# Moving one matrix-product piece, one weight unit and a few additions in a fused top-k attention and MLP kernel

## The chip, the core and the metric

The kernel runs on one core of a Trainium2 chip. The metric is the device time of one execution in microseconds (us). Beside the time of each execution there is a profile of one of them, taken by the hardware profiler; its span runs from the first to the last instruction.

The engines are called as in the profile: PE is the matrix engine (PEld its weight loads), DVE the vector engine, ACT the scalar engine, POOL the GpSimd engine, SP the engine that issues most DMAs.

## The reference: what is computed

For 8 batches and 8 heads, with 576 rows and a head dimension of 64, all in float32:

```
scores = q @ k.T / 8                       # 576 x 576 for each head
kth    = 32nd largest of each row
attn   = softmax(where(scores >= kth, scores, -1e9))
x      = (attn @ v), heads side by side    # 4608 x 512
out    = gelu(x @ w_in) @ w_out            # w_in 512 x 2048, w_out 2048 x 512, exact gelu
```

## The kernel before: how the work is tiled and ordered

**Items and slots.** The attention is cut into items. An item is one tile of 128 query rows for a pair of heads (both heads side by side, 2 x 576 scores per row). A batch has four head pairs and four full row tiles, which makes 16 full items, and two items that hold the leftover 64 rows of two pairs each. So there are N = 144 items. They are ordered so that two row tiles of a pair follow each other, then the next pair: after eight full items, 256 rows of x are complete over all heads. Even batches put their two leftover items behind the full ones, odd batches ahead of them.

The program is one loop over slots n (from line 1034). In slot n each engine gets, in this order of the program: the addition that completes a unit of weights (POOL), scores of item n+2 (in late slots of two items, n+2 and n+3, in every second slot), `attend(n-3)`, which is the product with v of two row tiles at once and so exists in every second slot, `copy_x`, which copies that product to `xT` on ACT, the softmax of item n-1 on ACT, the transposes of item n-2 on PE with the copies to `pt` on ACT, and the top-k of item n on DVE. At the end POOL computes the thresholds and normalises item n-1 (line 507); the transposes of the next slot need that. Every engine works through its own instructions in program order, so this order is the schedule. Every engine pair is tied only by data.

**The MLP in between.** The MLP runs in pieces that are strewn into the slots by `mlp(count)`. A piece is two matmuls 128x256 of a first layer block (`l1_piece`, line 673, tile `h_ps`), or one matmul 128x512 or two matmuls 128x256 of a second layer block (lines 755, 773/776, 809/811, tiles `y_ps` and `seven`). A first layer block has eight pieces, a second layer block seven or eight. `room_in(n)` says how many pieces slot n may take: 4 in all slots up to 11 (START is 10), later a block's size plus or minus one. A piece of the first layer has a `need`: the tokens of x that must be complete. `mlp` stops where `need` is above `ready[0]`, and `ready[0]` is raised to the finished tokens at fixed places of the slot. In a slot with a product that completes 256 tokens, the next first layer block is still blocked directly after the product. There the loop does something else: with `few[0]` (slots from 13) it issues the eight main transposes of item n-2 at once (`turned`, made by `turn_both`, line 553) and the small transposes of the leftover keys (`tails`, line 527), and only then raises `ready[0]`.

**The second layer** saves products by sums of quarters (one multiplication in eight is saved). `sums` (lines 699 to 708) makes three sums of the gelu result `g` and changes one quarter of `g` in place, in four POOL additions into one buffer `sum`; `trio_piece` and `seven_piece` use them. `last_parts` (line 881) adds up the last 256 rows of the output on DVE and stores them.

**The weights** come as 16 units. A unit is loaded by SP, taken apart on ACT (lines 205 and 206, and a multiplication by a constant, on ACT at line 212 or, for slots 11 to 18, on DVE at line 208) and added up on POOL (line 227) at the beginning of its slot. `SLOT_OF` gives the units, in the order `ORDER`, the slots 1 to 10 and 13 to 18. The size steps of a slot's unit are issued at the end of the slot before.

**At the beginning** the PE has little to do; `keep_busy` fills slots below 10 with matmuls on constants (line 995), whose results nobody reads. From slot 10 the MLP starts.

Of the kernel before, what the change touches and what calls it, by code (L numbers as in the profile page):

```python
# [14 lines left out]
def kernel(  # L15
# [19 lines left out]
    nc = tc.nc  # L35
    f32, i32, u32 = mybir.dt.float32, mybir.dt.int32, mybir.dt.uint32
# [5 lines left out]
    P = 128  # L42
# [115 lines left out]

    SLOT_OF = dict(zip(ORDER, [*range(1, START + 1), *range(START + 3, START + 9)]))
    UNIT_IN = {n: u for u, n in SLOT_OF.items()}
    unit_in = UNIT_IN.get

# [53 lines left out]
    def waits(u):  # L218

        return u == ORDER[-1]  # L220
# [104 lines left out]
    def pair_tile(name, tag="pr"):  # L325
        return ps.tile([P, 2, 512], f32, tag=tag, bufs=1, name=name)
# [31 lines left out]
    def scores(i, second=False):  # L358
        if i >= N or i in S_of:
            return  # L360
        pair, t = items[i]
        S_of[i] = s = work.tile([P, 2 * S], f32, tag="s", bufs=6, name="s")
        s_ps = pair_tile("s_ps", "l1" if second else "pr")
        if not few[0]:
            last_keys(i, bank("t_ps"))()
        if t < NM:
            q_t, kt = q_of[pair][:, t * P : (t + 1) * P], kt_of[pair]
            for e in range(2):
                rows = slice(e * D, (e + 1) * D)
                nc.tensor.matmul(  # L370
                    s_ps[:, e], lhsT=q_t[rows, :], rhs=kt[rows, 0:SM], start=True, stop=True
                )
            if i == 0:

                nc.scalar.activation(s[:, 0:SM], s_ps[:, 0], func=AF.Copy, scale=scale)
                nc.scalar.activation(s[:, S + TL :], s_ps[:, 1], func=AF.Copy, scale=scale)  # L376
                return
            nc.scalar.activation(spread(s, S + TL, SM), s_ps, func=AF.Copy, scale=scale)  # L378
        else:

            for r in range(2):
                kt = kt_of[pair + r]
                for e in range(2):
                    rows = slice(e * D, (e + 1) * D)
                    nc.tensor.matmul(
                        s_ps[half(r, e), r, :], lhsT=kt[rows, SM + P + e * TL : SM + P + (e + 1) * TL],
                        rhs=kt[rows, 0:SM], start=True, stop=True,
                    )
            s2 = s.rearrange("p (r n) -> p r n", r=2)
            nc.scalar.activation(s2[:, :, 0:SM], s_ps, func=AF.Copy, scale=scale)  # L390
# [122 lines left out]
    def transposes(i):  # L513

        if i < 0 or i >= N:
            return []
        t, s = items[i][1], S_of.pop(i)
        pr = [None]

        def tails(ahead):  # L520
            tp = bank("tp_t")
            keys = last_keys(ahead, tp) if ahead is not None and ahead < N else None
            at = P
            if t % 2 == 0:
                pt_now[0] = work.tile([P, 2 * NM + 1, 2 * P], f32, tag="pt", bufs=1, name="pt")
            if t < NM:
                nc.tensor.transpose(tp[:, at : at + P], s[:, SM : S + TL], ident)  # L527
            else:
                for r in range(2):
                    nc.tensor.transpose(  # L530
                        tp[0:TL, at + r * P : at + (r + 1) * P],
                        s[:, r * S + SM : (r + 1) * S], ident,
                    )
            if keys:
                keys()
            if t < NM:
                nc.scalar.copy(
                    out=pt_now[0][:, 2 * NM, t % 2 * P : (t % 2 + 1) * P], in_=tp[:, at : at + P]
                )
                return  # L540
            for e in range(2):
                c = slice(e * TL, (e + 1) * TL)
                nc.scalar.copy(
                    out=halves(pt_end[c, 0, :], e, P),
                    in_=halves(tp[0:TL, at : at + 2 * P], e, P),
                )

        x = t % 2 * P if t < NM else 0

        def turn_over(tp, e):  # L550
            first = e * (S + TL if t < NM else S)
            for j in range(NM):
                nc.tensor.transpose(  # L553
                    tp[:, j * P : (j + 1) * P], s[:, first + j * P : first + (j + 1) * P], ident
                )

        def main(e):
            tp = bank("tp")
            turn_over(tp, e)
            nc.scalar.copy(  # L560
                out=pt_now[0][:, e * NM : (e + 1) * NM, x : x + P],
                in_=tp.rearrange("p (j n) -> p j n", j=NM),
            )

        def turn_both():
            pr[0] = tp = pair_tile("tp")
            for e in range(2):
                turn_over(tp[:, e], e)

        def both():  # L570
            if pr[0] is None:
                turn_both()
            tp = pr[0]
            nc.scalar.copy(  # L574
                out=pt_now[0][:, 0 : 2 * NM, x : x + P],
                in_=tp.rearrange("p e (j n) -> p (e j) n", j=NM),
            )

        if few[0]:
            return [tails, lambda _: both(), turn_both]  # L580
        return [tails] + [lambda _, e=e: main(e) for e in range(2)]

    def copy_x():
        while copies:
            copies.pop()()
# [112 lines left out]
    def sums(u):  # L698

        g = g_of[u].rearrange("p x (f n) -> p x f n", f=2)  # L700
        a11, a21, a12, a22 = (g[:, :, f, h * P : (h + 1) * P] for f in range(2) for h in range(2))
        t = work.tile([P, 2, 3, P], f32, tag="sum", bufs=1, name="sum")
        s1, s2, s4 = (t[:, :, x] for x in range(3))
        nc.gpsimd.tensor_tensor(s1, a21, a22, op=ALU.add)
        nc.gpsimd.tensor_tensor(s2, s1, a11, op=ALU.subtract)
        nc.gpsimd.tensor_tensor(a21, a11, a21, op=ALU.subtract)
        nc.gpsimd.tensor_tensor(s4, a12, s2, op=ALU.subtract)
        sums_of[u] = t

    def weight_sums(j):  # L710
# [32 lines left out]
    def part_tile():  # L743
        return work.tile([P, HALF], f32, tag="part", bufs=3, name="part")
# [137 lines left out]
    def last_parts(tok, k, a):  # L882

        dve, add = nc.vector.tensor_tensor, ALU.add
        if k == 0:
            end_of["y"] = y0, y1 = y_tile(), y_tile()
            nc.scalar.copy(out=y0[:, B1], in_=a[:, 0])
            end_of["a"] = a
            return
        y0, y1 = end_of["y"]  # L890
        s7 = y7[0]
        if k == 1:
            dve(y0[:, B2], a[:, 0], y0[:, B1], op=add)
            dve(y0[:, B1], end_of["a"][:, 1], y0[:, B1], op=add)
            nc.sync.dma_start(out=out[last_row : last_row + P, B1], in_=y0[:, B1])
            dve(s7, s7, y0[:, B2], op=add)
            dve(y1[:, B2], a[:, 1], s7, op=add)
            nc.sync.dma_start(out=out[last_row + P : last_row + 2 * P, B2], in_=y1[:, B2])
            dve(y0[:, B2], a[:, 1], y0[:, B2], op=add)
            return  # L900
        dve(y0[:, B2], a[:, 1], y0[:, B2], op=add)
        nc.sync.dma_start(out=out[last_row : last_row + P, B2], in_=y0[:, B2])
        dve(y1[:, B1], s7, a[:, 0], op=ALU.subtract)
        nc.scalar.dma_start(out=out[last_row + P : last_row + 2 * P, B1], in_=y1[:, B1])
# [68 lines left out]
    def room_in(n):  # L973

        x = n - START - 1
        if x < 1:
            return 4
        if x >= len(sizes):
            return 0
        return sizes[x] + (1 if x % 2 == 0 else -1)  # L980
# [53 lines left out]
    for n in range(ahead):  # L1034

        left[0] = room_in(n)
        few[0] = n > START + 2
        eager[0] = n > N
        if not waits(unit_in(n)):
            weights_add(unit_in(n))  # L1040
        larger(n + 1)
        for piece in squares_in.pop(n, []):
            piece()
        two = few[0] and n % 2 == 0 and n + 3 < N and items[n + 3][1] < NM
        scores(n + 2, two)
        if two:
            scores(n + 3)
        product = attend(n - 3)
        late = n > START
        if n <= START:  # L1050

# [2 lines left out]
        if waits(unit_in(n)):  # L1054
            weights_size(unit_in(n))
            weights_add(unit_in(n))
        mlp(1)
        if few[0] and n % 2:
            run_gelus()
        tr = transposes(n - 2)  # L1060
        turned = tr.pop() if few[0] and tr else None
        if product and n > START and done[0] < len(pieces) and pieces[done[0]][0] > ready[0]:

            if turned:
                turned()
            for piece in tr[:1]:
                piece(n + 2 if few[0] else None)
            tr, ready[0] = tr[1:], n_tok[0]
# [103 lines left out]
```

## Time and profile before

| what | us |
|---|---|
| median of 3 runs (1547.71 to 1549.83) | 1548.0 |
| profiled execution, its own time | 1547.88 |
| its span, first to last instruction | 1546.1 |
| PE busy in the span | 1513.3 |
| DVE busy | 1336.4 |
| ACT busy | 1160.4 |
| POOL busy | 1142.8 |

A row of the timeline gives the start, the length, the engine, the line, the operation with the tiles that it writes and reads, its shape and a count, and in brackets how long the engine had been idle before and what released it. Consecutive equal instructions are merged into one row. A float32 matmul is recorded as two instructions, so a first layer piece of two matmuls shows as x4 in the trace. The time between two matmul rows is read from start to start, because the ends are modelled and overlap the next start.

### The profile page before, as it was taken

Reading aid. Unit: us, or ns where it says so; the run is one execution under the profiler, and the core shown is the slowest. Engines: PE = TensorE matmul, PEld = TensorE weight load, DVE = VectorE, ACT = ScalarE, POOL = GpSimd, SP = SyncE. Lnnn points to the kernel's source line nnn. Section 1 sums busy time; section 2 is a strip of 40 time slices with the busy share of each in tenths; the row PEclk is TensorE's granted clock in tenths of the full one; section 3 lists DMA queues with packets and bytes.
Section 4 is the critical chain, followed back from the end, with each engine's and each line's share of the span. In section 5 each row is a group of like instructions: output and inputs, shape, how many; then the busy total and the mean of one; then the engine's idle time right before and its main releaser. Section 6 shows DMA issues by size and latency. Waiting matters only on the chain. (4 is left out here: it accounts for less than half of the span.)

```text
span 1546.1 us, 28114 instructions
## 1 busy us (share of the span) xinstructions
PE 1513.3 (98%) x9240; PEld 1193.3 (77%) x9240; DVE 1336.4 (86%) x4583; ACT 1160.4 (75%) x2038; POOL 1142.8 (74%) x1291
## 2 busy tenths in 40 slices
PE   7899999999999999999999999999999999999998
PEld 5676577877777777888777778788778777788887
DVE  8999999989989988899989998988998998888700
ACT  6999987777777777777777777777777777787720
POOL 4896657777787868767787877776788787877732
PEclk9999999999999999999999999999999999999999
DMA  6424310012101110012201111011110111000000
GB/s 161 149 99 113 86 46 1 18 35 39 24 15 31 38 35 19 1 30 46 40 14 20 27 32 45 1 25 36 32 24 22 24 30 32 15 1 15 8 14 14
DMA packets 195027, 56.36 MB, mean 36 GB/s; under 512 B 185888, under 2 KB 186432, under 8 KB 194880
## 3 DMA queue, kind: packets, MB, share of 16 engines
q1 hardware_dynamic: 193616, 54.14, 14.9%
q8 instruction: 73, 1.20, 0.3%
q14 instruction: 74, 0.61, 0.1%
q10 hardware_dynamic: 1200, 0.39, 0.1%
q0 software_dynamic: 64, 0.03, 0.0%
HBM read 45.08 MB, written 9.44 MB: 35 GB/s over the span
## 5 line engine op out<-in xcount | busy, mean ns | idle before, releaser
L673 PE MATMUL h_ps<-xT,w_in_sb 128*128 128x256 f32 (+1 forms) x2560 | 539.6, 361 | 1.8 <-ACT xT L620 1.7
L673 PEld LDWEIGHTS h_ps<-xT,w_in_sb 128*128 128x128 f32 x2560 | 434.9, 191 | 73.5 <-issue 25.3
L450 DVE MAX8 top<-lists 128x8 f32<-128x288 f32 x792 | 321.4, 448 | 0.0
L507 POOL TENSOR_TENSOR s<-s,rden 128x1152 f32<-128x1152 f32 x144 | 302.9, 2104 | 0.3 <-DVE rden L482 0.3
L496 ACT ACTIVATE s<-s,bias 128x576 f32<-128x576 f32 x288 | 223.3, 775 | 11.9
L453 DVE MATCH_REPLACE8 lists<-top,lists 128x288 f32<-128x288 f32 x528 | 229.9, 443 | 0.0
L495 ACT ACTIVATE s<-s,neg 128x576 f32<-128x576 f32 x288 | 225.7, 784 | 2.9 <-POOL neg L475 2.8
L450 DVE MAX8 low<-lists 128x8 f32<-128x288 f32 x528 | 213.2, 446 | 0.0
L574 ACT COPY pt<-tp 128x1024 f32<-128x1024 f32 x133 | 134.9, 1014 | 95.9 <-PE tp L553 95.9
L488 POOL TENSOR_SCALAR den<-den 128x2 f32<-128x2 f32 x144 | 31.6, 219 | 224.6 <-ACT s L496 220.9
L421 POOL TENSOR_TENSOR lists<-lists 128x576 int32<-128x576 int32 x132 | 186.3, 1412 | 4.0
L413 POOL TENSOR_TENSOR lists<-s 128x576 int32<-128x576 int32 x132 | 185.9, 1408 | 0.0
L553 PE MATMUL tp<-ident,s 128*128 128x128 f32 x1152 | 150.4, 273 | 8.2 <-POOL s L507 8.2
L553 PEld LDWEIGHTS tp<-ident,s 128*128 128x128 f32 x1152 | 133.5, 141 | 27.9 <-POOL s L507 14.5
L615 PE MATMUL o<-pt,raw_v 128*64 128x256 f32 x1280 | 153.7, 385 | 0.4 <-ACT pt L560 0.4
L615 PEld LDWEIGHTS o<-pt,raw_v 128*64 128x64 f32 x1280 | 87.3, 137 | 86.1 <-issue 45.7
L475 POOL TENSOR_SCALAR neg<-kth 128x2 f32<-128x2 f32 x132 | 85.9, 651 | 90.6 <-DVE kth L466 90.0
L811 PE MATMUL y_ps<-w_out_sb,sum 128*128 128x256 f32 x480 | 142.8, 379 | 0.0
L378 ACT ACTIVATE s<-s_ps 128x1024 f32<-128x1024 f32 x127 | 124.2, 1025 | 15.1 <-PE s_ps L370 15.0
L370 PE MATMUL s_ps<-kt,qm 64*128 64x512 f32 x512 | 131.2, 626 | 0.8 <-ACT s L376 0.8
L482 DVE RECIPROCAL rden<-den 128x2 f32<-128x2 f32 x144 | 23.4, 162 | 124.0 <-POOL den L488 122.3
L453 DVE MATCH_REPLACE8 lists<-low,lists 128x288 f32<-128x288 f32 x264 | 115.0, 444 | 0.0
(148 smaller groups left out, 2771.3 us busy)
## 6 DMA issues: line engine op xcount, KB each, us to landing
raw_v<-in_v_dram SPq DMA_DIRECT2D x64, 128.0 KB, 2.3
out_dram<-y SPq DMA_DIRECT2D x30, 256.0 KB, 2.1
raw_q<-in_q_dram SPq DMA_DIRECT2D x112, 64.0 KB, 2.0
raw_k<-in_k_dram SPq DMA_DIRECT2D x112, 64.0 KB, 2.0
w_out_sb<-in_moe_w_in_dram SPq DMA_DIRECT2D x14, 511.8 KB, 4.7
w_out_sb<-in_moe_w_out_dram SPq DMA_DIRECT2D x10, 511.8 KB, 4.3
w_sum<-in_moe_w_out_dram SPq DMA_DIRECT2D x6, 511.8 KB, 4.2
raw_q<-in_q_dram SPq DMA_DIRECT2D x112, 8.0 KB, 1.8
```

What stands on the lines that cost most here:

```text
L413: nc.gpsimd.tensor_tensor(t[:, 1].bitcast(i32), a.bitcast(i32), b.bitcast(i32), op=ALU.add)
L421: nc.gpsimd.tensor_tensor(both, both, top, op=ALU.subtract)
L450: nc.vector.max(x[:, e], src[:, e])
L453: nc.vector.match_replace(dst[:, e], x[:, e], src[:, e], LOWEST)
L495: nc.scalar.activation(s, s, func=AF.Prelu, bias=st["neg"][:, e : e + 1], scale=1.0, alpha=STEEP)
L496: nc.scalar.activation(s, s, func=AF.Exp, bias=st["bias"][:, e : e + 1], scale=1.0, accum_out=st["den"][:, e : e + 1],)
L507: nc.gpsimd.tensor_tensor(s, s, wide, op=ALU.mult)
L553: nc.tensor.transpose(tp[:, j * P : (j + 1) * P], s[:, first + j * P : first + (j + 1) * P], ident)
L574: nc.scalar.copy(out=pt_now[0][:, 0 : 2 * NM, x : x + P], in_=tp.rearrange("p e (j n) -> p (e j) n", j=NM),)
L615: nc.tensor.matmul(o[e * D : (e + 1) * D, 0:n], lhsT=vt[:, j, e, :], rhs=pt[:, e * NM + j if j < NM else 2 * NM, :], start=(j == 0), stop= ...
L673: nc.tensor.matmul(h_tile(u)[:, i, :], lhsT=w_in_sb[:, ko, f * P : (f + 1) * P], rhs=xT[:, ko, c0 : c0 + n], start=(ko == 0), stop=(ko == ...
L811: nc.tensor.matmul(acc[names][:, k], lhsT=lhsT, rhs=rhs, start=(j == 0 and k == 0), stop=(j == FT // 2 - 1 and k == 1),)
```

## The change

Seven edits, in program order:

1. `SLOT_OF`: the tenth unit of weights (ORDER[9], unit 11, of w_out) moves from slot 10 to slot 11. Slot 11 lies in `ON_DVE`, so its multiplication runs on DVE (line 208) where before it ran on ACT (line 212).
2. `transposes`: `turn_both` is gone; in late slots the eight main transposes stand only in `both`, behind `tails`.
3. New `closes(i)`: true for the last full item of an odd row tile in the last pair of a batch, in late slots. In the slot where `attend(n-3)` is that item, the slot takes one MLP piece more and the slot before takes one less, and `ready[0]` is raised directly behind the first `mlp(1)`. So the last piece of the second layer block that was left over comes right behind the product with v, and then two pieces of the next first layer block, the small transposes, one more piece, and the main transposes. There are 15 such slots.
4. `sums` of the last unit pair (NU-2) runs on DVE into a buffer of the tag "s" that attention used, in place of POOL and the buffer `sum`.
5. `last_parts`: one of the DVE additions, and the store behind it, moves to the first of the three calls and writes to a tile of its own.
6. `room_in`: 6 pieces in slot 10 and 2 in slot 11, in place of 4 and 4.
7. In slot 10 the product with v and its copy to `xT` come ahead of the scores, and `ready[0]` is raised there.

The core of the diff:

```diff
-    SLOT_OF = dict(zip(ORDER, [*range(1, START + 1), *range(START + 3, START + 9)]))
+    SLOT_OF = dict(zip(ORDER, [*range(1, START), START + 1, *range(START + 3, START + 9)]))
...
-        def turn_both():
-            pr[0] = tp = pair_tile("tp")
+        def both():
+            tp = pair_tile("tp")
             for e in range(2):
                 turn_over(tp[:, e], e)
...
-            return [tails, lambda _: both(), turn_both]
+            return [tails, lambda _: both()]
...
+    def closes(i):
+
+        if not few[0] or i < 0 or i >= N:
+            return False
+        pair, t = items[i]
+        return t < NM and t % 2 == 1 and pair % NP == NP - 1
...
-        t = work.tile([P, 2, 3, P], f32, tag="sum", bufs=1, name="sum")
+        if u == NU - 2:
+            t = work.tile([P, 2 * S], f32, tag="s", bufs=6, name="sum_s")
+            t = t[:, 0 : 6 * P].rearrange("p (x k n) -> p x k n", x=2, k=3)
+            add = nc.vector.tensor_tensor
+        else:
+            t = work.tile([P, 2, 3, P], f32, tag="sum", bufs=1, name="sum")
+            add = nc.gpsimd.tensor_tensor
...
-            end_of["a"] = a
+            first = part_tile()
+            dve(first, a[:, 1], y0[:, B1], op=add)
+            nc.sync.dma_start(out=out[last_row : last_row + P, B1], in_=first)
...
-            dve(y0[:, B1], end_of["a"][:, 1], y0[:, B1], op=add)
-            nc.sync.dma_start(out=out[last_row : last_row + P, B1], in_=y0[:, B1])
...
         if x < 1:
-            return 4
+            return 2 if x == 0 else 6
...
+        left[0] += closes(n - 3) - closes(n - 2)
...
+        if n == START:
+            product = attend(n - 3)
+            copy_x()
+            ready[0] = n_tok[0]
         scores(n + 2, two)
         if two:
             scores(n + 3)
-        product = attend(n - 3)
+        if n != START:
+            product = attend(n - 3)
...
         mlp(1)
+        if closes(n - 3):
+            ready[0] = n_tok[0]
...
-        turned = tr.pop() if few[0] and tr else None
         if product and n > START and done[0] < len(pieces) and pieces[done[0]][0] > ready[0]:
 
-            if turned:
-                turned()
             for piece in tr[:1]:
```

More of the change, by code (lines that the diff above doesn't have):

```diff
@@ L517, in transposes @@
         t, s = items[i][1], S_of.pop(i)
-        pr = [None]
         def tails(ahead):
@@ L563, in main @@
             )
-        def turn_both():
-            pr[0] = tp = pair_tile("tp")
+        def both():
+            tp = pair_tile("tp")
             for e in range(2):
                 turn_over(tp[:, e], e)
[L570 to L573, printed above, removed]
             nc.scalar.copy(
@@ L701, in sums @@
         a11, a21, a12, a22 = (g[:, :, f, h * P : (h + 1) * P] for f in range(2) for h in range(2))
-        t = work.tile([P, 2, 3, P], f32, tag="sum", bufs=1, name="sum")
+        if u == NU - 2:
[5 more added lines that the diff above has]
+            add = nc.gpsimd.tensor_tensor
         s1, s2, s4 = (t[:, :, x] for x in range(3))
[L704 to L707, printed above, removed]
+        add(s1, a21, a22, op=ALU.add)
+        add(s2, s1, a11, op=ALU.subtract)
+        add(a21, a11, a21, op=ALU.subtract)
+        add(s4, a12, s2, op=ALU.subtract)
         sums_of[u] = t
```

## The prediction

> **What bounds the kernel now.** I read the page first, then the waits of PE, then the timeline at three places: slots 10 to 12, one of the 15 slots of edit 3, and the last 20 us.
>
> ```profile
> span 1546.1 us, 28114 instructions
> PE 1513.3 (98%) x9240; PEld 1193.3 (77%) x9240; DVE 1336.4 (86%) x4583; ACT 1160.4 (75%) x2038; POOL 1142.8 (74%) x1291
> ...
> PE tp L553 <- POOL s L507: 8.2, 13, 1.1
> ...
> PE seven L809 <- POOL g L706: 2.4, 1, 2.4
> ...
> PE tp_t L527 <- POOL s L507: 0.8, 4, 0.3
> ```
>
> PE is busy for 98% of the span. From slot 10 on it has no filler work any more, so what it does not wait for later is the floor, and the change can give only what PE waits. The waits (total, times, longest) in reach of the change are 8.2 us in 13 waits of the main transposes for POOL's normalisation, 2.4 us in one wait of the last `seven`, and two single waits near slot 10 (1.72 and 0.43 us, rows below). All sums below are against the profiled execution, 1547.88 us with a span of 1546.1; the median of the three runs, 1548.0, lies 0.1 above it.
>
> **Edits 2 and 3, the 15 slots.** One of them, on PE, ACT and POOL (start, length):
>
> ```profile
> 470.35 2.38 PE L615 MATMUL o<-pt,raw_v 128*64 128x256 f32 x20
> 471.67 2.10 POOL L507 TENSOR_TENSOR s<-s,rden 128x1152 f32<-128x1152 f32 x1
> 472.80 0.37 ACT L620 COPY xT<-o 128x256 f32<-128x256 f32 x1 [1.25 <-PE o L615]
> 473.83 1.09 PE L553 MATMUL tp<-ident,s 128*128 128x128 f32 x8 [1.10 <-POOL s L507]
> 475.09 7.07 PE L673 MATMUL h_ps<-xT,w_in_sb 128*128 128x256 f32 x32
> ...
> 1461.55 2.38 PE L615 MATMUL o<-pt,raw_v 128*64 128x256 f32 x20
> 1463.86 2.86 PE L673 MATMUL h_ps<-xT,w_in_sb 128*128 128x256 f32 x12
> ```
>
> PE finishes the product `o` and has nothing but the transposes, whose operand POOL completes at 473.77. Behind an undisturbed product the next matmul starts 2.31 us after the product's start (1461.55 to 1463.86); here it takes 3.48. So the wait costs 1.17, 0.07 more than its row says, and its transposes run 1.09 where others take 1.04: 0.12 more per wait, 1.6 over 13, together 9.8 us.
>
> After the change the same stretch is: scores 0.87 us earlier, since a piece has left the slot before (the row at 475.09 has 32 matmul records, eight pieces, in 7.07); `o` from 469.5 to 471.8; that piece, to 472.7; two first layer pieces, to 474.4; the small transposes (0.3 of the 1.26 between 473.83 and 475.09); one piece, to 475.6; then the main transposes, 1.8 us behind POOL's end. PE does the same matmuls, only in another order. The cover is the one piece behind the product: it lasts 0.87, and the first layer needs the copy to `xT`, which follows the end of the product by 0.07 and lasts 0.37, 0.5 with its signal. ACT is free for it: it waited 1.25 for the product before, and the scores that it copies ahead come earlier too. If the cover were gone, a wait of up to 0.5 would stand in each slot, 7.5 in all.
>
> Where a stall goes, the next one must be looked for. What is late next is the chain ACT, POOL, DVE, POOL that makes the next normalisation:
>
> ```profile
> 480.16 0.22 POOL L488 TENSOR_SCALAR den<-den 128x2 f32<-128x2 f32 x1
> ...
> 490.70 0.17 DVE L482 RECIPROCAL rden<-den 128x2 f32<-128x2 f32 x1 [0.68 <-POOL den L488]
> ...
> 513.44 2.11 POOL L507 TENSOR_TENSOR s<-s,rden 128x1152 f32<-128x1152 f32 x1
> 515.63 0.33 PE L527 MATMUL tp_t<-ident,s 128*128 128x128 f32 x1
> ```
>
> At 480.16 POOL had no wait: its own queue sets this time and does not come earlier. DVE at 490.70 had waited 0.68, so it can follow PE's 1.2 by 0.68 at most, and so can POOL's normalisation that ends at 515.55. PE's small transposes start 0.08 behind it, without slack. There about 0.5 of the 1.2 is lost again. The same place comes three times in the run, one period of two batches (365 us) apart. Elsewhere the small transposes wait only 0.8 us in 4 waits in all (first fence), and where DVE waits for ACT, as in most slots, the chain itself starts at PE and moves with it; there I count no loss. Bounds: nothing lost, 9.8; half of it lost again, 4.9. I take 9.8 - 1.5 = **8.3 us**.
>
> **Edits 4 and 5, the end.**
>
> ```profile
> 1527.43 1.09 ACT L689 ACTIVATE g<-h_ps 128x512 f32<-128x512 f32 x2 [11.60 <-PE h_ps L673]
> 1532.76 0.59 PE L811 MATMUL y_ps<-w_out_sb,sum 128*128 128x256 f32 x2
> 1533.53 0.72 POOL L704 TENSOR_TENSOR sum<-g 128x256 f32<-128x256 f32 x1 [9.37 <-PE y_ps L811]
> 1535.79 1.13 PE L809 MATMUL seven<-w_sum,g 128*128 128x256 f32 x4 [2.43 <-POOL g L706]
> 1540.56 0.42 DVE L893 TENSOR_TENSOR y<-y_ps,y 128x256 f32<-128x256 f32 x1 [68.87 <-PE y_ps L811]
> 1541.36 0.41 DVE L896 TENSOR_TENSOR y<-y,y 128x256 f32<-128x256 f32 x1
> 1541.50 0.59 PE L811 MATMUL y_ps<-w_out_sb,sum 128*128 128x256 f32 x2
> 1542.67 0.42 DVE L901 TENSOR_TENSOR y<-y_ps,y 128x256 f32<-128x256 f32 x1
> ```
>
> The last gelu ends at 1528.5, but POOL may not write the one `sum` buffer until the matmuls that read it are done, at 1533.35. With a buffer of its own on DVE, which idles for 68.87 us, the four additions take 4 x 0.41 = 1.64 (the row at 1541.36, also 128x256 from SBUF), until 1530.2. `seven` then follows the last matmul by 0.43 as other pieces do, at 1533.2 instead of 1535.79: **2.6 us**. The cover is 3 us long. Bounds of the additions: 0.41 to POOL's 0.72 each, hidden by either.
>
> A rule of the Trainium skill speaks against the move to DVE, and the trace has rows on it:
>
> ```profile
> 480.81 0.75 DVE L406 TENSOR_TENSOR lists<-s 128x576 f32<-128x576 f32 x1
> 480.97 0.66 POOL L475 TENSOR_SCALAR neg<-kth 128x2 f32<-128x2 f32 x1 [0.59 <-DVE kth L466]
> ...
> 1455.32 0.22 POOL L475 TENSOR_SCALAR neg<-kth 128x2 f32<-128x2 f32 x1 [0.59 <-DVE kth L466]
> ```
>
> The tiny POOL operation takes 0.66 beside the DVE addition of two tensors and ends with it; without one beside it, it takes 0.22. The Trainium skill, "SBUF — State Buffer", section "Who interferes with whom", says that a DVE instruction with two SBUF inputs and a GpSimd instruction that reads SBUF share one read port, and that the later one waits for the whole of the other. These rows agree. By that rule the four DVE additions would wait for the one POOL addition that stands there, by an estimate 0.7 us, which the cover of 3 us hides.
>
> Edit 5 takes one 0.42 addition out of the chain on DVE that starts at 1540.56 and ends behind PE's last matmul. The addition at 1542.67 could start when PE is done (1542.09); it is delayed 0.58 by the queue. So 0.4 of it goes: **0.4 us**, between 0 and 0.6. The store that moves on SP goes out earlier, with nothing queued behind it.
>
> **Edits 1, 6 and 7, slots 10 to 12.** These look as if they fill idle PE time. I follow ACT instead.
>
> ```profile
> 103.13 1.07 ACT L560 COPY pt<-tp 128x512 f32<-128x512 f32 x2
> 103.89 2.73 PE L615 MATMUL o<-pt,raw_v 128*64 128x256 f32 x20
> 104.08 1.29 ACT L205 ACTIVATE w_out_sb<-w_out_sb,high 128x1024 f32<-128x1024 int16 x1
> 106.58 1.16 ACT L212 ACTIVATE w_out_sb<-w_out_sb 128x1024 int32<-128x1024 uint32 x1
> 107.78 1.00 ACT L378 ACTIVATE s<-s_ps 128x1024 f32<-128x1024 f32 x1
> 110.70 0.70 PE L673 MATMUL h_ps<-xT,w_in_sb 128*128 128x256 f32 x2 [1.72 <-ACT xT L620]
> 121.15 0.56 ACT L560 COPY pt<-tp 128x512 f32<-128x512 f32 x1
> 121.76 2.37 PE L615 MATMUL o<-pt,raw_v 128*64 128x256 f32 x18 [0.43 <-ACT pt L560]
> 121.33 0.22 POOL L488 TENSOR_SCALAR den<-den 128x2 f32<-128x2 f32 x1 [2.46 <-ACT s L496]
> 131.56 0.69 DVE L208 TENSOR_SCALAR w_out_sb<-w_out_sb 128x1024 int32<-128x1024 uint32 x1
> 142.92 0.17 DVE L482 RECIPROCAL rden<-den 128x2 f32<-128x2 f32 x1 [0.75 <-POOL den L488]
> ...
> L496 ACT ACTIVATE s<-s,bias 128x576 f32<-128x576 f32 x288 | 223.3, 775 | 11.9
> L495 ACT ACTIVATE s<-s,neg 128x576 f32<-128x576 f32 x288 | 225.7, 784 | 2.9 <-POOL neg L475 2.8
> ```
>
> Before, PE waits 1.72 for `xT`, because the weight steps (104.08 to 107.7) and the score copy stand ahead of that copy on ACT. After, the product still waits for the second `pt` copy (104.2) and ends at 106.6, whatever stands ahead; `xT` is ready at 107.05 and the 1.72 goes. But scores come behind the product, ACT copies them at 108.05 (0.27 later than at 107.78), and then has two weight steps (2.5 us) ahead of slot 11, less the 1.16 that went to DVE. PE is done with the scores at 107.9; five pieces (4.3) and five transposes (0.6) later, at 112.8, come the last four transposes of slot 10. Their copy ends at 113.9, the weight steps at 116.4, the copies of the next scores (1.1) at 117.5; two softmax halves take 2 x (0.78 + 0.78), reading their sums and two copies 0.8, and the copy that PE waits for, at 121.15 before, starts at 121.4. PE arrives 1.1 us earlier and waits for it longer. So this is **0.3 us lost**. Bounds: PE's arrival decides, a gain of 1.1; ACT's lost 2.6 us in front of `xT` less the 1.16, a loss of 1.4. DVE's 0.69 goes through slots 11 and 12, where it waits for nothing, and is swallowed by its wait of 0.75 at 142.92. POOL's addition for the unit moves into the gap of 2.46 that POOL has at 121.33. SP's order of loads stays.
>
> **Sum:** -8.3 - 2.6 - 0.4 + 0.3 = -11.0; 1547.88 - 11.0 = 1536.9, so **1537.0** on the scale of the median.
>
> **Rivals.**
> *The stall moves one slot on.* More of the 13 gains end in waits of the small transposes (0.8 us in 4 waits now, slack 0.08 at 515.63). For it: POOL and DVE set their own time at 480.16. Against it: DVE has 14% of the span free. With half of 9.8 lost: 1537.0 + 3.4 = 1540.4.
> *All of it is kept* and PE decides in slot 12: 1537.0 - 1.5 - 1.4 = 1534.1.
> *Slower: the first layer now waits for `xT` in each of the 15 slots.* The product's copy would stand behind other ACT work. Against it: ACT waited 1.25 there; for it: the one 1.72 wait at 110.70 was of this kind. It decides from 0.37 us behind its forecast time on (0.87 less 0.5). To be slower by 3.1 us the 15 slots must lose 11.0 + 3.1 = 14.1, 0.94 each, a copy 1.3 us late. At 1.5 us late the time is 1537.0 + 15 x 1.13 = 1554.
> *The beginning costs more:* ACT's 1.4 in full and DVE's 0.69 not swallowed: 1537.0 + 1.8 = 1538.8; that alone changes no sign.
>
> **Chances.** Forecast, with the beginning's rival, 0.58 (1535.5 to 1539); stall moves on 0.18 (to 1542.5 if it takes nearly all); all kept 0.08 (1534); nearly nothing left of the 15 slots, only the end, 0.07 (1544.9 to 1548); slower by `xT` 0.09. The range 1534 to 1543 leaves out the last two, 0.16. A measurement can tell about 0.2% (3.1 us): faster 0.85, same 0.06, slower 0.09.
>
> **What would show it.** In the profile after: no wait of `tp` L552 for POOL's normalisation, and no new row of `h_ps` for `xT` over 0.2 us in late slots (edit 3); waits of the small transposes for POOL at three places near 515, 880 and 1245, of 0.3 to 0.5 (the loss); `seven` at the end without wait (edit 4); the last addition at most 1.5 us behind PE's end (edit 5); in slot 12 a wait of `o` for `pt` of 1 us or more (edits 1, 6, 7). It is wrong if these waits total over 5 us, or if the end of slot 12's product moves by over 1 us.

## The result and the profile after

| | median, us | lowest to highest | runs |
|---|---|---|---|
| before | 1548.91 | 1547.71 to 1549.86 | 6 |
| after | 1538.34 | 1536.24 to 1539.43 | 6 |

The ratio is 0.9931, with a 95% interval from 0.9918 to 0.9944: 10.6 us faster. The forecast was 1537.0, 11.0 us faster, with a range from 1534 to 1543. The profiled execution of after took 1539.43 us, its span is 1537.6.

The first lines of the page of after, and PE's waits (what waited and for what: us in total, times, longest):

```profile
span 1537.6 us, 28098 instructions
PE 1514.7 (99%) x9240; PEld 1193.6 (78%) x9240; DVE 1338.8 (87%) x4588; ACT 1158.8 (75%) x2037; POOL 1139.1 (74%) x1287
```
```profile
PE t_ps L333 <- ACT qm L286: 7.9, 4, 5.0
...
PE o L616 <- ACT pt L559: 2.4, 2, 1.4
...
PE tp_t L526 <- POOL s L507: 1.4, 6, 0.3
...
PE o L616 <- ACT pt L568: 0.2, 1, 0.2
```

The row of `tp` (8.2 us in 13 waits) is gone, and so are those of `seven` (2.4) and of `h_ps` for `xT`. The small transposes wait 1.4 us in 6 waits where it was 0.8 in 4. New are two waits of the product with v for `pt`, 1.04 in slot 10 and 1.40 in slot 12 (2.4 in 2 waits; it was 0.43 in slot 12 alone), and one of 0.2 near the end.

To see where the time went, I cut each span at five rows of PE's timeline: the start of slot 9's main transposes, the start of the rest (x18) of slot 12's product with v, the start of the last output piece ahead of the last `seven`, the start of that `seven`, and the span's end.

| stretch, us | before | after | difference | forecast |
|---|---|---|---|---|
| start to slot 9's transposes | 101.65 | 103.21 | +1.56 | 0 |
| to the product of slot 12 (edits 1, 6, 7) | 20.11 | 20.41 | +0.30 | +0.3 |
| to the last output piece (edits 2, 3) | 1411.00 | 1403.79 | -7.21 | -8.3 |
| to the last `seven` (edit 4) | 3.03 | 0.43 | -2.60 | -2.6 |
| to the end (edit 5) | 10.31 | 9.76 | -0.55 | -0.4 |

From slot 9 on the change gives 10.06 us in these two executions; the 1.56 at the top stand where the diff touches nothing, and are taken up with the last two experiments.

**One of the 15 slots** in the timeline of after, the one that the forecast showed at 470:

```profile
467.55 1.99 PE L370 MATMUL s_ps<-kt,qm 64*128 64x512 f32 x8
469.46 2.38 PE L616 MATMUL o<-pt,raw_v 128*64 128x256 f32 x20
471.65 2.10 POOL L507 TENSOR_TENSOR s<-s,rden 128x1152 f32<-128x1152 f32 x1
471.77 0.30 PEld L818 LDWEIGHTS y_ps<-w_sum,g 128*128 128x128 f32 x2 [0.39 <-issue]
471.77 0.70 PE L818 MATMUL y_ps<-w_sum,g 128*128 128x256 f32 x2
471.92 0.37 ACT L621 COPY xT<-o 128x256 f32<-128x256 f32 x1 [0.72 <-PE o L616]
472.31 0.59 PE L818 MATMUL y_ps<-w_out_sb,sum 128*128 128x256 f32 x2
472.74 1.89 PE L674 MATMUL h_ps<-xT,w_in_sb 128*128 128x256 f32 x8
...
475.66 1.04 PE L552 MATMUL tp<-ident,s 128*128 128x128 f32 x8
```

The order is the forecast's: the shifted output piece (471.77 to 472.74), first layer pieces, and the main transposes 1.9 us behind POOL's end at 473.75. One thing remains: from 471.77 to 472.31 are 0.54 where matmuls of this shape stand 0.43 apart (472.31 to 472.74), and PEld had been idle for 0.39. The first matmul behind the product still costs 0.11.

**Given back**, in the timeline of after:

```profile
514.85 0.33 PE L526 MATMUL tp_t<-ident,s 128*128 128x128 f32 x1 [0.29 <-POOL s L507]
...
877.76 0.33 PE L526 MATMUL tp_t<-ident,s 128*128 128x128 f32 x1 [0.27 <-POOL s L507]
...
1240.69 0.33 PE L526 MATMUL tp_t<-ident,s 128*128 128x128 f32 x1 [0.27 <-POOL s L507]
```

These are the three places, one period apart, that the forecast named (near 515, 880 and 1245). At the first of them POOL's normalisation ends at 514.79, 0.76 us earlier than before (515.55), while PE's scores ahead of it come 1.15 earlier (488.20, before 489.35). From 502.06 to 511.33 POOL goes from one operation to the next without a wait, so its own queue sets that time.

**The end**, in the timeline of after:

```profile
1523.19 0.42 DVE L711 TENSOR_TENSOR sum_s<-g 128x256 f32<-128x256 f32 x1 [57.16 <-ACT g L690]
1523.51 0.72 POOL L839 TENSOR_TENSOR y<-y,p 128x256 f32<-128x256 f32 x1 [4.71 <-ACT p L837]
1523.65 0.86 DVE L712 TENSOR_TENSOR sum_s<-sum_s,g 128x256 f32<-128x256 f32 x1
...
1524.77 0.41 DVE L714 TENSOR_TENSOR sum_s<-g,sum_s 128x256 f32<-128x256 f32 x1
...
1527.41 0.59 PE L818 MATMUL y_ps<-w_out_sb,sum 128*128 128x256 f32 x2
...
1527.84 1.03 PE L816 MATMUL seven<-w_sum,g 128*128 128x256 f32 x4
...
1534.99 0.37 ACTq L911 DMA_DIRECT2D out_dram<-y  x1
```

The sums are done at 1525.18, and `seven` follows the piece ahead of it by 0.43, with no wait. From its start to the issue of the last store on ACT's queue are 7.15 us; before it was 7.67 (1535.79 to 1543.46).

**Slots 9 to 12** in the timeline of after:

```profile
103.21 1.04 PE L552 MATMUL tp<-ident,s 128*128 128x128 f32 x8
105.28 2.86 PE L616 MATMUL o<-pt,raw_v 128*64 128x256 f32 x20 [1.04 <-ACT pt L559]
...
108.18 0.37 ACT L621 COPY xT<-o 128x256 f32<-128x256 f32 x1 [2.46 <-PE o L616]
109.67 1.02 ACT L378 ACTIVATE s<-s_ps 128x1024 f32<-128x1024 f32 x1 [0.79 <-PE s_ps L370]
115.64 1.27 ACT L205 ACTIVATE w_out_sb<-w_out_sb,high 128x1024 f32<-128x1024 int16 x1
116.94 1.26 ACT L206 ACTIVATE w_out_sb<-w_out_sb,low 128x1024 int32<-128x1024 f32 x1
...
123.00 0.56 ACT L559 COPY pt<-tp 128x512 f32<-128x512 f32 x1
...
123.62 2.37 PE L616 MATMUL o<-pt,raw_v 128*64 128x256 f32 x18 [1.40 <-ACT pt L559]
```

PE's old wait for `xT` is gone, but the product, which no longer has scores ahead of it, waits 1.04 for `pt`, ACT now idles 2.46 us ahead of that copy and 0.79 ahead of the scores, and the two weight steps (115.64 to 118.2) stand in slot 11. The `pt` copy that the next product needs ends at 123.56, 20.35 behind slot 9's transposes, where before it was 20.06 (121.71 less 101.65).

### The profile page after: what moved, and what is told of

The parts are those of the page before. It is cut to its first block, busy times and chain, and to the rows that moved or that the text cites. A ratio compares the mean times of both kernels' runs of the same rounds, so it can differ in the third digit from the quotient of the medians.

```text
span 1537.6 us, 28098 instructions
## 1 busy us (share of the span) xinstructions
PE 1514.7 (99%) x9240; PEld 1193.6 (78%) x9240; DVE 1338.8 (87%) x4588; ACT 1158.8 (75%) x2037; POOL 1139.1 (74%) x1287
## 4 chain that ended last, share of the span: by engine, by line
PE 74%; POOL 11%; DVE 5%; ACT 1%; issue 1%; DVEq 0%; POOLq 0%
PE h_ps L674 27%; PE y_ps L818 15%; PE o L616 8%; PE tp L552 6%; PE s_ps L370 6%; POOL s L507 3%; PE seven L816 2%; PE y_ps L762 2%; PE y_ps L780 2%; PE y_ps L783 2%; POOL lists L413 1%; POOL lists L421 1%; DVE lists L453 1%; PE tp_t L333 1%; PE o L627 1%; DVE top L450 1%
```

## The experiments

The theory for all of them is the forecast's sum, term by term; each experiment sets a rival against one term. The first four were timed beside the same 20 runs of the kernel before (median 1549.78), with 5, 10, 11 and 5 runs of their own.

**The three parts alone, and all but one.** The kernel before with edits 2 and 3 only, of which this is the core:

```diff
+        left[0] += closes(n - 3) - closes(n - 2)
...
         mlp(1)
+        if closes(n - 3):
+            ready[0] = n_tok[0]
```

> The kernel before with edits 2 and 3 alone (the 15 slots). Theory: each slot gives what its wait row in the profile of before says plus 0.02 us (8.5 in all), and three later waits of the small transposes take back 0.35 each: 7.4 us faster, 1541.5 against a median of 1548.9. As the prediction counted it (0.12 more per wait, 0.5 lost three times): 8.3 faster, 1540.6. Rival: the 15 slots gave only what the two other groups of edits don't explain if the beginning gained 1.1 us: 6 us faster, 1543. In the profile the last 256 rows' wait of seven (2.4 us) must still be there.

The kernel before with edits 4 and 5 only:

```diff
+        if u == NU - 2:
+            t = work.tile([P, 2 * S], f32, tag="s", bufs=6, name="sum_s")
...
+            first = part_tile()
+            dve(first, a[:, 1], y0[:, B1], op=add)
```

> The kernel before with edits 4 and 5 alone (the end). Theory: 2.6 us for the wait of the last seven and 0.55 for the end of the addition chain, 3.1 faster, 1545.8. Rival: the end is set by the stores, and the moved addition is worth nothing: 2.6, 1546.3. In the profile the time from the start of the last seven to the end of the span is 9.8 by the theory, 10.3 by the rival.

The kernel before with edits 1, 6 and 7 only:

```diff
-    SLOT_OF = dict(zip(ORDER, [*range(1, START + 1), *range(START + 3, START + 9)]))
+    SLOT_OF = dict(zip(ORDER, [*range(1, START), START + 1, *range(START + 3, START + 9)]))
...
-            return 4
+            return 2 if x == 0 else 6
...
+        if n == START:
+            product = attend(n - 3)
+            copy_x()
+            ready[0] = n_tok[0]
```

> The kernel before with edits 1, 6 and 7 alone (slots 10 to 12). Theory: ACT sets when slot 12's product can go on; 0.3 us slower, not to be told from 1548.9 in the times, but in the profile the time from slot 9's main transposes to the rest of slot 12's product is 20.4 us against 20.1 before. Rival: PE's arrival decides, 1.1 us faster, 19.0 in the profile.

The changed kernel with these three edits undone (the same diff, backwards):

> The changed kernel without edits 1, 6 and 7. Theory: 0.3 us faster than the changed kernel, 1538.0, with 20.1 us from slot 9's main transposes to the rest of slot 12's product. Rival: the three edits bring 1.1, so 1539.4 without them.

| kernel | median, us | ratio to before | slot 9 to 12 | to the last piece | to `seven` |
|---|---|---|---|---|---|
| edits 2, 3 | 1542.99 | 0.9962 (0.9949 to 0.9974) | 20.09 | 1403.71 | 3.03 |
| edits 4, 5 | 1545.76 | 0.9976 (0.9967 to 0.9985) | 20.04 | 1410.79 | 0.43 |
| edits 1, 6, 7 | 1549.93 | 1.0002 (0.9993 to 1.0011) | 20.38 | 1411.03 | 3.03 |
| all but 1, 6, 7 | 1537.62 | 0.9927 (0.9915 to 0.9939) | 20.07 | 1403.68 | 0.43 |

The stretches are those of the table above, each from the profile of that kernel. Each part moves its own stretch, and the others by at most 0.21. The 15 slots gave 7.29, as this theory had it (7.4) and not the prediction (8.3) or the rival (6); with edits 4 and 5 alone the time from the last `seven` to the end is 9.82, the theory's 9.8 and not the rival's 10.3. The medians are looser. They add up, -6.8, -4.0 and +0.15 to -10.7 where it was -10.6 together, but their intervals are 2.8 to 3.9 us wide. The beginning's +0.3 shows in the profiles; in the times it drowns.

**What the last wait did to the clock.** One stretch is not in this table: from the start of the last `seven` to the end it is 10.31 in before, but 13.05 with edits 2 and 3 and 11.93 with edits 1, 6 and 7, where the same code stands and `seven` waits the same 2.43 us. PE's rows behind that wait, in before and then with edits 2 and 3, and the windows of both (stretch, its length, PE busy, clock, DMA share, GB/s):

```profile
1536.76 1.89 PE L811 MATMUL y_ps<-w_out_sb,g 128*128 128x256 f32 x8
```
```profile
1529.15 1.55 PE L810 MATMUL seven<-w_sum,g 128*128 128x256 f32 x4 [2.43 <-POOL g L707]
1530.49 3.20 PE L812 MATMUL y_ps<-w_out_sb,g 128*128 128x256 f32 x8
```
```profile
1536.00:1540.00 4.00, 4.00 (x20) 1.00 0.02 4
```
```profile
1530.00:1532.00 2.00, 2.00 (x6) 0.50 0.00 0
```

With edits 2 and 3 the clock fell to 0.50 behind the wait, and from the start of `seven` to that of the last piece PE took 7.40 us in place of 5.71; with edits 1, 6 and 7 it was 0.50 too, and 7.34. (With edits 2 and 3 the end came 1.05 later still; these lie behind the issue of the last store, 3.69 in place of 2.64.) So the wait that edit 4 removes cost 2.4 us in one profiled execution and some 1.6 more in two others. The one profile of before shows the cheap case. How many of its executions had the dear one no profile shows; that its times lie in two groups (1547.5 to 1548.3 and 1549.6 to 1551.2, while those with edits 4 and 5 lie between 1544.5 and 1546.7) and that edits 4 and 5 gave 4.0 in the medians where their stretches give 2.60 and 0.49 would fit, but is not a proof.

**The cover taken away.** The changed kernel without the shift of a piece, so that the first layer piece stands directly behind the product:

```diff
-        left[0] += closes(n - 3) - closes(n - 2)
```

> The changed kernel without the shift of one piece (the line that adds to left and takes from it): in the 15 slots the first layer follows the product directly. Theory: it then waits for the copy to xT, about 0.5 us behind the product's end, in each slot; from the rest of slot 12's product to the last piece of the second layer ahead of the last seven it takes 6 to 7.5 us more than the 1403.8 of the changed kernel, 1410 to 1411, and the wait list has h_ps for xT 15 times. Rival: raising ready alone is what helps and the shifted piece is not needed: 1404 and no such waits.

One execution took 1538.46 us, and the stretch to the last piece 1403.47, 0.32 shorter than with the cover. The same slot in its timeline:

```profile
469.69 2.38 PE L616 MATMUL o<-pt,raw_v 128*64 128x256 f32 x20
...
472.00 1.99 PE L674 MATMUL h_ps<-xT,w_in_sb 128*128 128x256 f32 x8
472.14 0.37 ACT L621 COPY xT<-o 128x256 f32<-128x256 f32 x1 [1.25 <-PE o L616]
```

The first layer piece starts at 472.00, ahead of the copy at 472.14 that I thought it needed, and has no wait; the list of PE's waits has none of `h_ps` for `xT`. The loop over `ko` in `l1_piece` says why: the copied part of `xT` holds the last quarter of the columns of x, and a first layer block goes through the quarters in order. Its first piece reads quarters 0 and 1, its second piece 2 and 3, so that the fourth matmul is the first one to read the new quarter. At 0.43 a matmul that is 1.3 us behind 472.00, and the copy is done at 472.51. So it is the earlier raising of `ready`, with the main transposes moved behind (edit 2), that takes the wait away. The shift adds nothing and costs a little: of the 0.32, 0.24 is a wait of a product with v for `pt` (1472.76 in after), which this kernel does not have.

**Buffer or engine.** The changed kernel with the last sums back on POOL, still in the buffer of their own:

```diff
-            add = nc.vector.tensor_tensor
+            add = nc.gpsimd.tensor_tensor
```

> The changed kernel, with the four additions of the last unit pair back on POOL, but still in the buffer of their own. Theory (the buffer ended the wait, not the engine): the last gelu ends at 1523.2, POOL needs its one other addition and four sums, 5 x 0.72 = 3.6 us, and is done at 1526.8, a us ahead of PE; so the last seven still starts 0.43 us behind the piece ahead of it, and the time stays at 1538.4 within 1.5. Rival (DVE was needed, because POOL is late there as well): the seven has a wait of 0.5 us or more for POOL, up to the 2.4 of before, and the time rises by as much, to 1540.8.

In the timeline of this kernel, the four additions on POOL:

```profile
1523.32 0.72 POOL L711 TENSOR_TENSOR sum_s<-g 128x256 f32<-128x256 f32 x1 [4.44 <-ACT g L690]
...
1525.48 0.73 POOL L714 TENSOR_TENSOR sum_s<-g,sum_s 128x256 f32<-128x256 f32 x1
```

They are done at 1526.2, and `seven` starts at 1527.92, 0.43 behind the piece ahead of it. One execution took 1539.90, with the same stretches as after to within 0.05 (20.41, 1403.74, 0.43). It was the buffer; DVE adds nothing.

**Which of edits 1, 6 and 7 costs.** Each undone alone in the changed kernel: the tenth unit back in slot 10, the pieces back to four and four, the scores ahead of the product again.

```diff
-    SLOT_OF = dict(zip(ORDER, [*range(1, START), START + 1, *range(START + 3, START + 9)]))
+    SLOT_OF = dict(zip(ORDER, [*range(1, START + 1), *range(START + 3, START + 9)]))
```

> The changed kernel with the tenth unit of weights back in slot 10 (edit 1 undone, 6 and 7 kept). Theory (ACT's queue sets when slot 12's product goes on): the three weight steps fill the time in which ACT waits for the product, and nothing stands ahead of slot 11's scores; from slot 9's main transposes to the rest of slot 12's product 19.5 us against 20.4. Rival (PE's extra pieces are the cost): still 20.4.

```diff
-            return 2 if x == 0 else 6
+            return 4
```

> The changed kernel with four pieces each in slots 10 and 11 again (edit 6 undone, 1 and 7 kept). Theory: the last transposes of slot 10 come 1.7 us earlier and the weight steps start up to 1.4 earlier, but the transposes of slot 11 come later; 19.7 us from slot 9's main transposes to the rest of slot 12's product. Rival (edit 6 is without effect): 20.4.

```diff
-        if n == START:
-            product = attend(n - 3)
-            copy_x()
-            ready[0] = n_tok[0]
...
-        if n != START:
-            product = attend(n - 3)
+        product = attend(n - 3)
```

> The changed kernel with the product behind the scores in slot 10 again (edit 7 undone, 1 and 6 kept). Theory: ACT copies the scores while the product runs and loses no time, 18.6 us from slot 9's main transposes to the rest of slot 12's product; but the DVE, with its 0.69 us more, is then the next that PE waits for, about 0.6 us at the small transposes of slot 12. Rival (the unit in slot 11 is the cost wherever the product is): 20.4.

| undone in the changed kernel | one time, us | slot 9 to 12 | to the last piece |
|---|---|---|---|
| nothing (after) | 1539.43 | 20.41 | 1403.79 |
| 1, the unit's slot | 1538.62 | 19.51 | 1403.75 |
| 6, the pieces | 1537.48 | 19.71 | 1403.87 |
| 7, product first | 1536.81 | 18.33 | 1403.97 |

The rest of slot 12's product, in the timeline of each, in the order of the table:

```profile
122.86 2.37 PE L616 MATMUL o<-pt,raw_v 128*64 128x256 f32 x18 [0.65 <-ACT pt L559]
```
```profile
121.59 2.37 PE L616 MATMUL o<-pt,raw_v 128*64 128x256 f32 x18 [0.83 <-ACT pt L559]
```
```profile
107.65 0.33 PE L526 MATMUL tp_t<-ident,s 128*128 128x128 f32 x1 [0.28 <-POOL s L507]
...
120.74 2.37 PE L616 MATMUL o<-pt,raw_v 128*64 128x256 f32 x18 [0.65 <-ACT pt L559]
```

In all three the product still waits for ACT, only less, as the theory of ACT's queue said, and within 0.3 of its figures. The wait of 0.6 that the theory expected at slot 12's small transposes with edit 7 undone did not come. The 0.28 in the first row of the last fence is in slot 10, where the kernel before has it too (0.29 at 106.92). Each of the three edits alone makes this stretch longer beside the two others, edit 7 by 2.08, of which 1.04 is the wait of slot 10's product. With edit 7 undone the two other edits bring 1.7 (20.07 with none of the three, 18.33).

**The unit one slot further.** The changed kernel with the tenth unit in slot 12:

```diff
-    SLOT_OF = dict(zip(ORDER, [*range(1, START), START + 1, *range(START + 3, START + 9)]))
+    SLOT_OF = dict(zip(ORDER, [*range(1, START), START + 2, *range(START + 3, START + 9)]))
```

> The changed kernel, with the tenth unit of weights in slot 12 in place of slot 11. Theory (ACT's queue ahead of the product of slot 12 decides the beginning): the two size steps, 2.53 us on ACT, no longer stand ahead of the pt copy that this product waits for, the copy ends 2.5 us earlier and PE, which arrives 1.40 us before it today, decides: the wait of 1.40 is gone and the stretch from slot 9's transposes to the rest of slot 12's product is 19.0 us in place of 20.4. The steps then stand ahead of slot 12's softmax, which may give back some of it behind this product, up to 1 us. Rival (PE's own work or POOL decides there): the stretch stays at 20.2 or more.

```profile
121.65 2.37 PE L616 MATMUL o<-pt,raw_v 128*64 128x256 f32 x18 [0.65 <-ACT pt L559]
...
143.30 1.09 PE L385 MATMUL s_ps<-kt 64*64 64x512 f32 x8 [1.54 <-ACT pt L568]
```

One execution took 1539.25 us. The stretch fell to 19.45, not 19.0: without the weight steps ACT itself has to wait for PE's transposes and scores, and 0.65 of the 1.40 stays. And 1.54 come back two slots later, where the weight steps now stand ahead of other copies; the next stretch is 1405.58, 1.8 longer. The theory was right on the place, wrong on the sum: I had allowed 1 us to come back.

**Why the executions differ at the start.** Slot 9's transposes start between 101.57 and 103.35 in the profiles of all the kernels above, also where nothing ahead of them was changed. In after, the granted clock and PE's rows there (windows: stretch, its length, PE busy, clock, DMA share, GB/s):

```profile
44.00:48.00 4.00, 0.65 (x4) 0.76 1.04 322
48.00:52.00 4.00, 2.31 (x6) 0.50 0.09 21
52.00:56.00 4.00, 4.00 (x20) 0.50 0.00 0
```
```profile
49.69 0.79 PE L333 MATMUL t_ps<-kt,qm 128*128 128x128 f32 x2 [5.04 <-ACT qm L286]
...
52.42 4.27 PE L616 MATMUL o<-pt,raw_v 128*64 128x256 f32 x20
```

PE waits 5.04 us for ACT's copy `qm`, the clock falls to 0.50, and the product that follows takes 4.27 us. In the kernel before, the clock of 52 to 56 us was 0.85 and this product took 2.78; with all but edits 1, 6, 7 it was 0.87 and 2.68, with edits 4 and 5 alone 0.65 and 3.74. These 1.49 between after and before are nearly all of the 1.56 in the table of stretches. So I filled the gap in the changed kernel:

```diff
-        if n == 1:
-            keep_busy(8, ident)
+        if n == 1 or n == 3:
+            keep_busy(8 if n == 1 else 18, ident)
```

> The changed kernel with 18 more fill matmuls (128x128, on constants, read by nobody) at the end of slot 3, where PE idles for 5.0 us until ACT has copied qm. Theory (the length of the beginning hangs on when the granted clock comes back after that idle time): the clock stays at 1.00 from 44 to 52 us, the product with v that follows takes 2.4 us in place of 2.7 to 4.3, slot 9's transposes start at 101.4 or earlier in the profile, and the median falls by 0.3 to 1.9 us, I take 1.1, to about 1537.3. Rival (the beginning differs between executions for another reason, a DMA or the order on ACT): the product at 52 us gets short, but slot 9's transposes still start anywhere from 101.6 to 103.4, and the median stays within 0.3 of the changed kernel's 1538.3.

The same views of this kernel:

```profile
44.00:48.00 4.00, 4.00 (x37) 1.00 0.99 314
48.00:52.00 4.00, 2.97 (x21) 1.00 0.04 9
52.00:56.00 4.00, 4.00 (x36) 1.00 0.00 0
```
```profile
44.34 4.18 PE L1002 MATMUL warm<-ident 128*128 128x128 f32 x36
49.55 0.49 PE L333 MATMUL t_ps<-kt,qm 128*128 128x128 f32 x2 [1.03 <-ACT qm L286]
...
51.03 2.38 PE L616 MATMUL o<-pt,raw_v 128*64 128x256 f32 x20
```

The clock stays up, the product takes 2.38, and slot 9's transposes start at 101.10. Four runs took 1537.27 to 1537.50 (median 1537.40; ratio to the before timed beside it, 1548.59, 0.9928, from 0.9911 to 0.9944). The spread is 0.23 us in four runs where the changed kernel had 3.19 in six. Its median is 0.9 lower than the changed kernel's, but the intervals of the two ratios overlap almost wholly, and the fastest execution of the changed kernel was 1536.24, faster than any of these; what it did otherwise no profile shows. So the clock, the shorter product and the smaller spread are shown, the gain in the median is not.

**The best of both.** The changed kernel with edit 7 undone and the same fill (both diffs are above):

> The changed kernel with edit 7 undone (slot 10 issues the scores ahead of the product again) and with the 18 fill matmuls at the end of slot 3. Theory (the two stand at different places and add): slot 9's transposes start at 101.1 as with the fill alone, the stretch from there to the rest of slot 12's product is 18.3 in place of 20.4 and the stretch behind it 0.2 longer, as with edit 7 undone alone; so 1537.4 - 2.1 + 0.2 = 1535.5 us, with a spread of less than 0.5 between executions. Rival (a later start hid part of it: with slot 9 earlier, ACT or POOL sets the product of slot 12): 0.5 to 1.5 of the 2.1 is not seen, and the time is 1536 to 1537.

Four runs took 1536.01 to 1536.32, median 1536.18; the ratio to before (1549.86 there) is 0.9910, from 0.9894 to 0.9927. It is the fastest median of all, 2.2 us under the changed kernel's, though the intervals of the two ratios overlap. It is 0.7 over the theory's 1535.5 and lies in the rival's range. But the stretch from slot 9 to 12 is 18.33 as expected, so the rival's mechanism, that something else would set it, is not what happened. What is missing stands elsewhere: slot 9's transposes start at 101.79, not 101.10, and the stretch to the last piece is 1404.18 where 1403.94 were expected. For the first the profile shows a second dip of the clock, to 0.79 between 20 and 28 us (0.85 before, 0.86 after, but 1.00 in the kernel with the fill alone). I did not try to fill that one.

## Why the prediction was right, step by step

- **Edits 2 and 3, the gain of 9.8: mis-sized, 8.5.** Aligned by the starts of the score matmuls, 13 of the 15 slots gain their row of idle time and 0.02 each, 8.2 + 0.3 = 8.5. I had counted 0.12 each, 0.07 for the first matmul behind the product and 0.05 for slower transposes. The first of them stays, as the 0.54 in place of 0.43 shows: it belongs to the matmul behind the product and not to the wait.
- **What is given back, 1.5: 1.05 at the places named.** Between score matmuls the three places lose 0.37, 0.35 and 0.33, 0.5 having been taken. The mechanism (POOL's own queue sets the normalisation's end) was right. The new wait of 0.24 for ACT at 1472.76 was not foreseen; it comes with the shifted piece. Together 7.2 and not 8.3: these sizes made the forecast of the 15 slots 1.1 us too good.
- **The cover of 0.87 for `xT`: wrong, and without effect on the sum.** The step read that the first layer needs the copy at its first matmul. It needs it at its fourth. So the rival that ends slower could not have come at the price that it was given. In after the fourth matmul behind 472.74 starts at 474.03 and the copy is done at 472.29: it could come some 1.7 us later before a slot lost anything, not 0.37.
- **Edit 4: right, 2.6 in the two profiles.** What the prediction did not have is the clock: the same wait was followed by a clock of 0.50 in two other profiles and cost 1.6 to 1.7 more there. The rule of the Trainium skill that the prediction weighed ("SBUF — State Buffer", "Who interferes with whom") shows: the DVE addition at 1523.65 takes 0.86 in place of 0.42, beside POOL's at 1523.51. That is 0.44 us lost, hidden as expected by the cover, of which 2.7 us were left.
- **Edit 5: right.** 0.52 from `seven` to the last store's issue, 0.4 forecast. With edits 4 and 5 alone it is 7.15 too. From that issue to the span's end it is 2.64 before, 2.61 in after and 2.67 with edits 4 and 5 alone, so the stores themselves changed nothing here.
- **Edits 1, 6 and 7: right, +0.3**, and by the mechanism given, ACT's queue ahead of a `pt` copy. PE's wait there is 1.40, as foreseen (over 1).
- **The rivals.** The stall did move on, at three places only. The beginning did not cost more than 0.3.
- **The span** fell by 8.5 only, not 10.1, since the start of the profiled execution of after was 1.56 longer, by the clock's return and not by the change. From slot 9 on it is 10.06. The medians, with their 10.6, take in the executions of before whose clock fell at the end as well, if there are such. The forecast had neither effect of the clock, so that its 11.0 lies this close to 10.6 is in part luck: by the stretches it was 0.9 too good.

## What to carry to other kernels

When a wait is to be covered, look up which instruction is the first to read the awaited data: here it was the fourth of its block, and the simple reordering was enough. The price of a removed wait is at least its idle row; what the first matmul behind a switch costs stays with whichever comes next, and what a lowered clock costs behind the wait goes with it, so look at the granted clock there in more than one execution. An edit that fills idle time of one engine must be followed on the others: three edits that seemed to help PE at the beginning lost, through ACT's queue, what two of them would have gained alone.

## What the runs showed of the hardware

- An idle time of PE of 4.1 to 5.1 us in the ramp of the kernel made the product with v behind it 0.3 to 1.9 us longer, another amount in each execution: the matmuls behind the idle time run at a granted clock of 0.50 until the clock is back, and this product took 2.68 to 4.27 us, against 2.38 at full clock. By the mean clocks of the windows (0.87 from 52 to 56 us with all but edits 1, 6 and 7; 0.50, and 0.96 from 56 to 60, in after) I estimate that the full clock came back 3.3 to 6.6 us after the first matmul at 49.7, if it goes from 0.50 to 1.00 in one step. The Trainium skill, "TensorE: Matmul & The Clock Gate", Part 1 and "HAM oscillation", says that the clock is set by a free-running window of about 3.4 us and halves after an idle window; the 0.50, the differences between executions and the cure by 4.2 us of fill matmuls agree with it, but a wait of 2.43 us, shorter than such a window, was enough at the end of the kernel.
- The same wait of 2.43 us ahead of the last `seven` left the clock at 1.00 in one profile (before) and was followed by 0.50 in two (edits 2 and 3; edits 1, 6 and 7). With edits 2 and 3 the mean clocks are 0.86, 0.50 and 0.72 from 1529 to 1530, to 1532 and to 1534; from these I estimate 3.4 us at 0.50, and the matmuls there took 1.69 us longer.
- The first matmul of 128x128 weights behind a product with 128x64 weights took 0.11 us longer than in a running chain: 0.54 to the next start in place of 0.43 (`y_ps`, 471.77), and 1.99 in place of 1.89 for four matmuls of `h_ps` (472.00 without the cover, 472.74 in after). Its weight load is not ahead of it (PEld idle 0.39).
- One DVE addition beside a POOL addition took 0.86 in place of 0.42.
